# Ungated weight loads, half tile loads as single steps, first v ahead of the identities, and a written-out order in an RWKV-5 attention and squared-ReLU kernel

## The chip, the cores and the metric

One core of a Trainium2 chip. The metric is device time in microseconds, from the start to the end of one execution; lower is better.

## The reference

```python
# r, k, v: (4, 8, 768, 48) f32; w, u: (8, 48); moe_w_in: (384, 2048); moe_w_out: (2048, 384)
state = zeros((B, H, D, D))
for t in range(S):
    cur = einsum('bhd,bhe->bhde', u * k[:, :, t], v[:, :, t])
    y[:, :, t] = einsum('bhd,bhde->bhe', r[:, :, t], state + cur)
    state = w[:, :, None] * state + einsum('bhd,bhe->bhde', k[:, :, t], v[:, :, t])
x = y.transpose(0, 2, 1, 3).reshape(B * S, H * D)     # 3072 x 384
out = (relu(x @ moe_w_in) ** 2) @ moe_w_out           # 3072 x 384
```

A linear attention with a decaying state, and behind it a two-layer network with a squared ReLU.

## The kernel before

The sequence is cut into 6 chunks of 128 positions. A unit is one chunk of one of the 4 batches, so there are 24 units, numbered chunk by chunk: unit i is chunk i // 4 of batch i % 4. A chunk's attention is done by matrix products instead of the recurrence. The steps of a unit, by the names of the program's planner:

- `rt`, `kt`, `vt`: loads of the unit's tile of r, k and v (192 KB each). The loads of r and k are issued by SP, those of v by POOL. For units 0 to 5 the tiles of r and k come in two halves with longer rows.
- `scale` (DVE, L458 and L460): r and k times powers of w, into the padded tile rkw.
- `turn` (PE transposes, L487) and `rkT` (ACT copies, L494), or from unit 6 on one transposing DMA (L476): rkT. `kb` (PE, L502, then ACT) turns k back for units 0 to 5. `vb` (ACT, L471) casts v.
- `rk` (DVE, L513), `at` (PE, L521) and `mask` (DVE, L533): the scores. `s` (called `sums` in the old code; PE, L541 and L546): the diagonal sums and the unit's share of the state. `dv`, `sadd`, `sdec` (DVE) and `stb` (ACT): diagonal term and state.
- `y` (PE, L576 and L582), `yb` (DVE, L591): the unit's y. `xturn` (PE, L607) and `xT` (ACT, L611), or from unit 6 on a transposing DMA (L600): x turned.
- `m1(i, s)` (PE, L623): quarter s of x @ w_in for unit i, 12 matmuls; needs quarter s of w_in, called I0 to I3 here. `relu` (ACT, L631), `sq` (ACT L638 or DVE L640). `m2(i, q)` (PE, L647): quarter q of the second product, 4 matmuls; needs quarter q of w_out, O0 to O3. `osb` (ACT, L654), `out` (SP): result and store.

Every weight quarter is loaded by POOL with a cast to bf16 (384 KB as bf16). Before its issue, POOL makes a one-column copy (`gate`, L442) of a tile of r or k that it is gated by, so the issue waits until that tile has landed: I0 by kt(2), I1 by rt(2), I2 by rt(4), I3 by kt(3), O3 by kt(4), O0 by rt(3), O1 by rt(4), O2 by kt(2). v(i) is gated in the same way by kt(i - 1) from unit 2 on (L465). POOL also makes the two identity matrices, at the very start (before the first v), the mask (`upper`), zeros, and the columns for u and the state's decay (`uwb`, `wend`).

The order on each engine is found when the program is built: `Plan` holds each step with an engine, a cost, a rank and the steps that it needs, and walks through a modelled time, giving each engine the step of lowest rank that is ready. It also gives out the 8 PSUM banks, and puts short matmuls on a constant tile (`fill`, L380) where PE would have nothing to do early on, 98 of them. Each engine then carries out its list in order.

On POOL the order is: v0, upper, v1, zeros, uwb, v2, I0, v3, I1, wend, I3, I2, v4, O0, O1, O2, O3, v5, v6 and so on. On PE, the order around the first products is: turn(3,1), m1(0,0), s(2), m1(1,0), y(2), kb(3), turn(4,0), at(3), s(3), xturn(2), m1(0,1), m1(1,1), m1(2,1), y(3), m1(2,0), turn(4,1), m1(0,3), ... and the second product begins m2(0,0), m1(3,1), m1(3,2), xturn(4), m2(1,0), m2(0,1), ..., m2(0,2), m1(4,3), m2(1,1), m2(1,2), m2(0,3).

Of the kernel before, what the change touches and what calls it, by code (L numbers as in the profile page):

```python
# [16 lines left out]
class Plan:  # L17

    def __init__(self, lags, cold, spare, turns):
        self.turns = turns
        self.lags = lags
        self.cold = cold  # L30
        self.spare = spare
        self.steps = []
        self.at = {}
        self.users = {}
        self.place = {}

    def add(self, key, engine, cost, emit, needs=(), rank=0.0, new=(), uses=(), move=None):
        kind, which = (key[0], key[1] if len(key) == 2 else key[1:]) if isinstance(key, tuple) else ("", key)
        rank = self.turns.get(kind, {}).get(which, rank)
        s = dict(key=key, engine=engine, cost=cost, emit=emit, rank=rank, new=new, move=move)  # L40
        s["needs"] = [n for n in needs if n is not None]
        self.at[key] = s
        self.steps.append(s)
        for x in tuple(new) + tuple(uses):
            self.users.setdefault(x, []).append(s)

    def run(self, room, banks, count):
        todo = {}
        for s in self.steps:
            todo.setdefault(s["engine"], []).append(s)  # L50
        for mine in todo.values():
            mine.sort(key=lambda s: s["rank"])
        rings = {name: [] for name in room}
        free = {e: 0.0 for e in todo}
        queues = {e: [] for e in todo}
        held = {n: None for n in range(count)}
        since = {n: 0.0 for n in range(count)}
        begin, until, tight, loose = self.spare
        free["SP"] = 0.74
        held[0] = "fill"  # L60
        order = []
        t = 0.0
        left = len(self.steps)
        tiny = 1e-9

        moved, chained, left_pe, to_pe, near = self.lags

        def ready(s, e):
            if s["move"]:
                return s["end"] + moved + s["move"][4]  # L70
            if s["engine"] == "PE":
                return s["end"] + (chained if e == "PE" else left_pe)
            return s["end"] + (to_pe if e == "PE" else near)

        marks = []

        def mark(s):
            for e in ("PE", ""):
                heappush(marks, ready(s, e))

        def done(s, e):
            return "end" in s and ready(s, e) <= t + tiny

        def fits(s):
            e = s["engine"]
            names = [x[0] for x in s["new"]]
            for name in set(names):
                if name in banks:
                    continue
                ring, m = rings[name], room[name]  # L90
                for n in range(len(ring) - m, len(ring) - m + names.count(name)):
                    if n >= 0 and not all(done(x, e) for x in self.users[ring[n]]):
                        return False
            wanted = [name for name in names if name in banks]
            if wanted:
                for n, x in held.items():
                    if x not in (None, "fill") and all(done(u, e) for u in self.users[x]):
                        held[n], since[n] = None, max(u["end"] for u in self.users[x])
                if sum(x is None for x in held.values()) < len(wanted):
                    return False  # L100
                for name in set(wanted):
                    mine = sum(x is not None and x[0] == name for x in held.values())
                    if mine + wanted.count(name) > banks[name]:
                        return False
            return True

        while left:
            if held[0] == "fill" and t > until:
                held[0] = None
            for e, mine in todo.items():  # L110
                if free[e] > t + tiny:
                    continue
                if e == "PE" and t < begin - tiny:
                    free[e] = begin
                    continue
                for s in mine:
                    if s["move"] and sum(x[1] / x[0]["move"][0] * x[0]["move"][3] for x in queues[e]) > 1.5:
                        continue
                    if all(done(self.at[k], e) for k in s["needs"]) and fits(s):
                        mine.remove(s)  # L120
                        left -= 1
                        for x in s["new"]:
                            if x[0] in banks:
                                n = 4 + x[1] if x[0] == "log" else min((n for n in held if held[n] is None), key=lambda n: since[n])
                                held[n] = x
                                self.place[x] = n
                            else:
                                rings[x[0]].append(x)
                        s["start"] = t
                        free[e] = t + s["cost"] * (self.cold[1] if e == "PE" and t < self.cold[0] else 1.0)  # L130
                        if s["move"]:
                            queues[e].append([s, s["move"][0], free[e] + s["move"][2]])
                        else:
                            s["end"] = free[e]
                            mark(s)
                        order.append(s)
                        break
                else:
                    if e == "PE" and t < until:
                        free[e] = t + (tight * self.cold[1] if t < self.cold[0] else loose)  # L140
                        order.append(dict(key="fill", emit=self.fill, start=t, end=free[e], engine="PE"))
            heads = [q[0] for q in queues.values() if q]
            moving = [x for x in heads if x[2] <= t + tiny]
            whole = sum(x[0]["move"][1] for x in moving)
            later = [f for f in free.values() if f > t + tiny]
            while marks and marks[0] <= t + tiny:
                heappop(marks)
            later += marks[:1]
            later += [x[2] for x in heads if x[2] > t + tiny]
            later += [t + x[1] * whole / x[0]["move"][1] for x in moving]  # L150
            if not later:
                if left:
                    raise ValueError("nothing can go on: " + str([s["key"] for m in todo.values() for s in m[:3]]))
                break
            step = min(later) - t
            t += step
            for x in moving:
                x[1] -= step * x[0]["move"][1] / whole
                if x[1] <= 1e-7:
                    queues[x[0]["engine"]].pop(0)  # L160
                    x[0]["end"] = t
                    mark(x[0])
        return order
# [3 lines left out]
def kernel(  # L167
# [26 lines left out]
    LATE = (0.2, 0.2, 0.4)  # L194
    MOST = 3
    SQUARES = 'AAAMAAAM'
    TURNS = {
        "": {
            "zeros": 38.551
        },  # L200
        "O": {
            0: 76.019, 1: 91.228, 2: 107.535, 3: 7
        },
        "rt": {
            0: -83.003, 1: -66.162, 12: 22.377, 13: 28.231, 14: 28.49, 15: 33.657, 3: -36.29, 5: 1.476, 8: 3.237
        },
        "kt": {
            0: -80.584, 1: -55.486, 10: 19.508, 11: 20.529, 2: -47.443, 6: 2.358
        },
        "at": {  # L210
            0: -3.958, 11: 34.671, 4: -16.745, 7: 10.944
        },
        "mask": {
            (1, 0): -39.238, (10, 0): 33.02, (2, 1): 25.375, (5, 1): 1.515
        },
        "sadd": {
            1: 9.124, 4: 45.244
        },
        "rk": {
            2: 13.012, 7: 14.32, 8: 68.867, 9: -12.042  # L220
        },
        "sums": {
            11: 49.353, 2: -24.778, 8: 5.082
        },
        "dv": {
            2: -26.848, 7: 34.164, 9: -12.993
        },
        "stb": {
            2: -9.741, 4: 57.421
        },  # L230
        "scale": {
            (10, 0): 23.594, (11, 0): -15.371, (3, 0): -29.763, (4, 0): 33.082, (7, 1): 6.517, (8, 1): 4.379
        },
# [656 lines left out]
```

## Time and profile before

| | |
|---|---|
| time, median of 3 runs | 175.78 us (175.55 to 176.24) |
| span of the profiled execution | 174.3 us (its own time beyond the span is not given; the median stands 1.5 us above the span) |
| PE busy | 166.7 us, 96% |
| ACT / DVE / POOL busy | 132.1 / 121.1 / 40.0 us |
| granted TensorE clock | 1.000 |
| DMA | 28.93 MB; HBM read 20.50 MB, written 4.72 MB |

How to read the lines of the profile: times are microseconds from the start of the span. In the chain of waits, each line is a start, a length, and what the chain was in. In a timeline, a line is a start, a length, the engine and line, the operation with the output and the inputs, and in brackets the idle time before it and what ended it. A row of the busy time by stretches is the stretch, its length, then the busy time and the count of instructions of PE, PEld (weight loads), DVE, ACT and POOL, then the clock, the DMA share and GB/s. A row of a DMA queue is its number of packets, megabytes written, and the time of its packets as a share of the 16 DMA engines' time in the stretch; shares of two queues can sum to over 100%. q0 is POOL's queue, q1 that of SP. "DMA to landing" is the time from an issue to its last byte, the three numbers being equal where the stretch holds a single issue.

### The profile page before, as it was taken

Reading aid. Unit: us, or ns where it says so; the run is one execution under the profiler, and the core shown is the slowest. Engines: PE = TensorE matmul, PEld = TensorE weight load, DVE = VectorE, ACT = ScalarE, POOL = GpSimd, SP = SyncE. Lnnn points to the kernel's source line nnn. Section 1 sums busy time; section 2 is a strip of 40 time slices with the busy share of each in tenths; the row PEclk is TensorE's granted clock in tenths of the full one; section 3 lists DMA queues with packets and bytes.
Section 4 is the critical chain, followed back from the end, with each engine's and each line's share of the span. In section 5 each row is a group of like instructions: output and inputs, shape, how many; then the busy total and the mean of one; then the engine's idle time right before and its main releaser. Section 6 shows DMA issues by size and latency. Waiting matters only on the chain.

```text
span 174.3 us, 5795 instructions
## 1 busy us (share of the span) xinstructions
PE 166.7 (96%) x2390; PEld 134.7 (77%) x2390; DVE 121.1 (70%) x252; ACT 132.1 (76%) x268; POOL 40.0 (23%) x84
## 2 busy tenths in 40 slices
PE   7978899999999999999999999999999999999991
PEld 6766799887687787886896787869787698877871
DVE  7869976615999899977986799794989635531010
ACT  3946999999458797886968876939994869948640
POOL 7866890300140220302032202203202000000000
PEclk9999999999999999999999999999999999999999
DMA  4889999999999999999999999999999971130121
GB/s 97 228 179 246 232 218 193 185 221 118 170 201 164 178 154 209 200 214 170 231 142 183 156 237 214 218 177 141 186 200 175 271 180 26 26 111 6 47 81 56
DMA packets 76474, 28.93 MB, mean 166 GB/s; under 512 B 65440, under 2 KB 75296, under 8 KB 76448
## 3 DMA queue, kind: packets, MB, share of 16 engines
q1 hardware_dynamic: 70848, 20.56, 69.8%
q0 software_dynamic: 5312, 7.87, 23.9%
q8 instruction: 18, 0.29, 0.8%
q10 hardware_dynamic: 288, 0.15, 0.4%
q14 instruction: 8, 0.07, 0.1%
HBM read 20.50 MB, written 4.72 MB: 145 GB/s over the span
## 4 chain that ended last, share of the span: by engine, by line
PE 81%; DMA 11%; SPq 4%; issue 1%; DVE 0%; POOL 0%; POOLq 0%
PE bank L623 35%; PE bank L647 33%; DMA w_in_q<-in_moe_w_in_dram 5%; SPq L436 4%; DMA rkT<-rkw 4%; PE bank L521 4%; DMA rt<-in_r_dram 2%; PE bank L576 2%; PE bank L582 2%; PE bank L546 2%; PE bank L663 2%; PE bank L541 1%; PE bank L487 0%; PE bank L607 0%; POOL gate L442 0%
## 5 line engine op out<-in xcount | busy, mean ns | idle before, releaser
L623 PE MATMUL bank<-xT,w_in_q 128*128 128x128 bf16 x1152 | 70.7, 219 | 0.1
L623 PEld LDWEIGHTS <-w_in_q 128*128 128x128 bf16 x1152 | 66.5, 98 | 3.1 <-DMA w_in_q<-in_moe_w_in_dram 0.3
L647 PE MATMUL bank<-w_out_q,g 128*128 128x384 bf16 x368 | 66.9, 326 | 0.0
L631 ACT ACTIVATE gr<-bank 128x512 f32<-128x512 f32 x96 | 54.3, 599 | 13.6 <-PE bank L623 13.3
L647 PEld LDWEIGHTS <-g 128*128 128x128 bf16 x368 | 33.3, 98 | 19.8
L638 ACT ACTIVATE g<-gr 128x512 bf16<-128x512 f32 x72 | 43.7, 637 | 0.4
L533 DVE TENSOR_TENSOR am<-bank,smask 128x512 bf16<-128x512 f32 x48 | 31.3, 682 | 3.3 <-PE bank L521 3.1
L640 DVE TENSOR_TENSOR g<-gr 128x512 bf16<-128x512 f32 x24 | 16.5, 686 | 21.5 <-ACT gr L631 21.5
L465 POOL COPY gate<-kt 128x1 f32<-128x1 f32 x22 | 5.8, 266 | 80.9 <-DMA kt<-in_k_dram 80.9
L654 ACT COPY osb<-bank 128x384 f32<-128x384 f32 x23 | 11.0, 483 | 15.8 <-PE bank L647 15.8
L467 POOL DMA_DIRECT2D vt<-in_v_dram x24 | 21.4, 893 | 5.9 <-issue 1.6
L555 DVE TENSOR_TENSOR dv<-vb,bank 128x384 f32<-128x384 bf16 x24 | 13.2, 548 | 5.3 <-PE bank L546 3.4
L513 DVE TENSOR_TENSOR rk<-rkT 128x512 bf16<-128x512 bf16 x24 | 10.0, 417 | 7.7 <-DMA rkT<-rkw 4.3
L591 DVE TENSOR_TENSOR yb<-bank,dv 128x384 bf16<-128x384 f32 x24 | 13.2, 550 | 2.8 <-PE bank L582 2.4
L471 ACT CAST vb<-vt 128x384 bf16<-128x384 f32 x24 | 12.4, 518 | 0.0
L458 DVE TENSOR_TENSOR rkw<-rt,wpos 128x384 bf16<-128x384 f32 x18 | 9.8, 550 | 1.4 <-DMA rt<-in_r_dram 1.4
L458 DVE TENSOR_TENSOR rkw<-kt,wneg 128x384 bf16<-128x384 f32 x18 | 9.9, 549 | 0.9 <-DMA kt<-in_k_dram 0.9
L567 ACT CAST stb<-st 128x384 bf16<-128x384 f32 x20 | 10.4, 519 | 0.0
L380 PE MATMUL bank<-warm 128*128 128x128 bf16 x98 | 9.3, 248 | 1.1 <-DVE warm L322 1.1
L521 PE MATMUL bank<-rkT 64*128 64x128 bf16 x192 | 9.5, 219 | 0.2
L494 ACT COPY rkT<-bank 128x512 bf16<-128x512 bf16 x12 | 6.8, 588 | 3.0 <-PE bank L487 3.0
L563 DVE TENSOR_TENSOR st<-st,wend 128x384 f32<-128x384 f32 x16 | 8.8, 549 | 0.0
(74 smaller groups left out, 129.1 us busy)
## 6 DMA issues: line engine op xcount, KB each, us to landing
vt<-in_v_dram POOLq DMA_DIRECT2D x24, 192.0 KB, 4.6
out_dram<-osb SPq DMA_DIRECT2D x23, 192.0 KB, 4.0
rt<-in_r_dram SPq DMA_DIRECT2D x18, 192.0 KB, 4.5
kt<-in_k_dram SPq DMA_DIRECT2D x18, 192.0 KB, 4.3
w_in_q<-in_moe_w_in_dram POOLq DMA_DIRECT2D x4, 384.0 KB, 7.9
w_out_q<-in_moe_w_out_dram POOLq DMA_DIRECT2D x4, 384.0 KB, 12.7
kt<-in_k_dram SPq DMA_DIRECT2D x12, 96.0 KB, 4.3
rt<-in_r_dram SPq DMA_DIRECT2D x11, 96.0 KB, 4.2
```

Source lines behind the costliest of these rows:

```text
L458: nc.vector.tensor_tensor(t["rkw"][:, x, :, :, :D], pair(src), pair(wneg if x else wpos), ALU.mult)
L467: nc.gpsimd.dma_start(out=tiles[i]["vt"], in_=v[b, :, c * C : (c + 1) * C, :].rearrange("h s d -> s h d"))
L471: nc.scalar.copy(tiles[i]["vb"], tiles[i]["vt"])
L521: nc.tensor.matmul(out=t["at"][o][:, p, :], lhsT=t["rkT"][sl, 1, p, :], rhs=t["rkT"][sl, 0, p, :], start=True, stop=True,)
L533: nc.vector.tensor_tensor(am, t["at"][o], smask.unsqueeze(1).to_broadcast([C, HP, C]), ALU.mult)
L555: nc.vector.tensor_tensor(t["dv"], t["vb"], t["d"].unsqueeze(2).to_broadcast([C, H, D]), ALU.mult)
L591: nc.vector.tensor_tensor(t["yb"], t["y"], t["dv"].rearrange("p h d -> p (h d)"), ALU.add)
L623: nc.tensor.matmul(out=t["h", s][:, a], lhsT=turned, rhs=chunks[c]["xT"][:, n, b : b + m, :], start=(n == 0), stop=(n == NK - 1),)
L631: nc.scalar.activation(t["gr", s], t["h", s], AF.Relu)
L638: nc.scalar.activation(g, x, AF.Square)
L640: nc.vector.tensor_tensor(g, x, x, ALU.mult)
L647: nc.tensor.matmul(out=t["o"], lhsT=chunks[units[i][0]]["g"][:, f, units[i][1], :], rhs=w_out_q[f // 4][:, f % 4, :], start=(f == 0), stop ...
```

## The change

- The planner is gone. The order of all steps is written out in a table of words, each step with the PSUM bank or banks that it takes (`m1.0.0@4`); each engine runs its words in the order of the table. 99 fills stand in it.
- The weight quarters have no gates. The order on POOL is v0, v1, the identities, I3, upper, I0, zeros, I2, uwb, wend, I1, v2, v3, O0, O3, O1, v4, v5, O2, v6 and so on. v is gated by the k before it from unit 6 on (`VGATE`), not from unit 2 on.
- A half tile load of r or k is a step of its own (`kt.0.0`), so that halves of different tiles can stand in any order: kt(0) comes first on SP, then rt(0,0), rt(1), rt(2), kt(1,1), kt(2), rt(3) and so on. kt(1,0) is issued from ACT's queue.
- The identities are made behind v(0) and v(1) on POOL, not ahead of them.
- On PE, unit 0 takes its four quarters early: turn(2,1), m1(0,0), s(1), kb(2), y(1), turn(3,0), at(2), m1(0,3), m1(0,2), turn(3,1), xturn(1), m1(0,1), at(3), kb(3), m1(1,2), m1(1,3), y(2), s(2), m1(1,1), y(3), s(3), turn(4,0), turn(4,1), m1(1,0), m2(0,0), xturn(3), at(4), xturn(2), kb(4), m1(3,0), ... m2(1,0), ... m2(1,1), y(4), turn(5,1), s(4), m2(0,1), m1(2,3), m2(1,2) ... Ahead of m1(0,0) stand turn(1,1), at(1), xturn(0) and kb(1). Later units' steps are also reordered throughout, for example unit 18's first product behind that of unit 21. Counts of steps ahead of and behind a step, here and below, are taken from the two orders.

```diff
+ORDER = """
+kt.0.0 kt.0.1 rt.0.0 rt.1.0 vt.0 rt.1.1 fill.25 log@4567 ktA.1.0 lnat.0 vt.1 rt.2.0 lnat.1 w.0 rt.2.1 ids w.1
+scale.0.0 kt.1.1 wk scale.0.1 I.3 kt.2.0 wr fill.16 turn.0.0@1 upper kt.2.1 turn.0.1@2 rkT.0.0 cols@3 scale.1.0
+rt.3.0 vb.0 I.0 copied rkT.0.1 rt.3.1 fill.6 turn.1.0@4 zeros vb.1 rk.0 kt.3.0 fill.6 kb.0@5 rkT.1.0 I.2 at.0@67
+kbT.0 kt.3.1 scale.2.0 uwb end mask.0.0 kt.4.0 fill.12 turn.2.0@1 mask.0.1 kt.4.1 wend rkT.2.0 scale.1.1 fill.8
+s.0@3 fill.1 y.0@2 dv.0 I.1 fill.4 turn.1.1@4 sadd.0 rt.4.0 rkT.1.1 vt.2 yb.0 stb.0 rk.1 rt.4.1 fill.14 at.1@56
+scale.2.1 vt.3 xturn.0@7 mask.1.0 kb.1@1 xT.0 rt.5.0 fill.2 turn.2.1@3 O.0 kbT.1 mask.1.1 rkT.2.1 fill.5 m1.0.0@4
+O.3 scale.3.0 rt.5.1 s.1@2 rk.2 relu.0.0 kb.2@7 O.1 sadd.1 y.1@5 rt.6 turn.3.0@1 kbT.2 at.2@06 dv.1 sqA.0.0 vt.4
...
+"""
-class Plan:
...
-    ident4 = const.tile([HP, HP], F32)
-    make_identity(nc, ident4)
...
+    def identities():
+        make_identity(nc, ident4)
+        make_identity(nc, identb)
...
-    def load(i, name):
+    def load(name, i, o=None, queue=None):
...
+        if o is None:
+            nc.sync.dma_start(out=t[name], in_=src.rearrange("h s d -> s h d"))
+        else:
+            (queue or nc.sync).dma_start(out=t[name][:, o * 4 : o * 4 + 4].rearrange("p l d -> p (l d)"), in_=halves(src)[o])
-    def weights(gated, q, which):
-        nc.gpsimd.tensor_copy(gate, tiles[gated[1]][gated[0]][:, H - 1, :1])
+    def weights(which, q):
...
     def load_v(i):
-        if i > 1:
+        if i >= VGATE:
             nc.gpsimd.tensor_copy(gate, tiles[i - 1]["kt"][:, H - 1, :1])
...
+    for word in ORDER.split():
+        what, _, where = word.partition("@")
+        name, *a = what.split(".")
+        if name == "fill":
+            for _ in range(int(a[0])):
+                fill()
+            continue
+        a = [int(x) for x in a]
+        if where:
+            place.update(zip(names(name, *a), (int(x) for x in where)))
+        steps[name](*a)
```

More of the change, by code (lines that the diff above doesn't have):

```diff
@@ L1 @@
 from contextlib import ExitStack
-from heapq import heappop, heappush
 import concourse.bass as bass
@@ L14 @@
 PSUM = bass.MemoryType.PSUM
-class Plan:
[L27 to L163, printed above, removed]
@@ new lines @@
+vb.6 kt.8 xturn.4@2 sqD.2.3 at.5@43 xT.4 m2.1.3 vt.7 scale.6.1 sqA.2.0 mask.5.1 m1.3.1@1 vb.5 osb.1 mask.5.0 m2.0.3
+rkD.6 sqA.3.0 scale.8.0 out.1 m2.2.0@5 relu.3.1 stb.4 y.5@7 osb.0 m2.2.1 scale.7.1 vt.8 sqA.3.1 out.0 m2.3.0@2 rkD.7
+vb.7 m2.2.2 s.5@3 kt.9 m2.3.1 dv.5 m1.4.0@0 sadd.5 vt.9 scale.8.1 m1.4.3@4 relu.4.0 sdec.5 m1.4.2@1 yb.5 sqA.4.0
+rk.6 rkD.8 at.6@63 relu.4.3 xturn.5@0 vb.8 mask.6.0 m2.3.2 relu.4.2 sqD.4.3 m2.3.3 xT.5 mask.6.1 stb.5 m2.2.3 osb.3
+sqA.4.2 m1.5.2@7 rt.9 osb.2 m2.4.0@4 out.3 relu.5.2 out.2 y.6@6 vb.9 rk.7 rt.10 at.7@10 sqA.5.2 m1.5.0@3 mask.7.0
@@ L166 @@
+osb.20 m2.18.1 out.20 m2.18.2 m2.18.3 m2.22.0@5 osb.18 m2.22.1 out.18 m2.22.2 m2.22.3 m2.23.0@1 osb.22 out.22
+m2.23.1@2 osb.23.0 out.23.0 osb.23.1 out.23.1
+"""
 @with_exitstack
@@ L300, in bank @@
             banks.extend([late.tile([128, 512], F32, name=f"bank{n}") for n in range(4, 8)])
-        return banks[plan.place[key]]
+        return banks[place[key]]
     ET = mybir.EngineType
@@ L331 @@
     ident4 = const.tile([HP, HP], F32)
-    make_identity(nc, ident4)
+    identb = const.tile([128, 128], BF16)
     which = const.tile([128, 2], I32)
@@ L683, in store @@
         nc.sync.dma_start(out=out[b * S + c * C : b * S + (c + 1) * C, :], in_=tiles[i]["osb"])
-    PE, ACT, DVE, POOL, SP = "PE", "ACT", "DVE", "POOL", "SP"
-    L1, L2 = 7, 18
-    def late(n, i):
-        return min(MOST, LATE[n] * max(0, i - NPE))
-    def do(fn, *a):
-        return lambda: fn(*a)
-    add = copy = plan.add
-    plan.fill = fill
-    add("w0", ACT, 3.2, None, rank=-1e3)
-    add("log", PE, 0.28, spread_log, rank=-1e3, needs=["w0"], new=[("log", n) for n in range(4)])
-    for x in range(2):
-        add(("lnat", x), DVE, 0.47, do(log_at, x), rank=-1e3 + x, needs=["w0", ("lnat", 0) if x else None])
-        add(("w", x), ACT, 0.42, do(power_four, x), rank=-1e3 + x, needs=[("lnat", x)])
@@ L704 @@
-    add("wk", ACT, 0.48, do(power, wneg, down), rank=-999, needs=["log", ("w", 1)], uses=[("log", n) for n in range(4)])
-    add("wr", ACT, 0.48, do(power, wpos, up), rank=-998, needs=["wk"], uses=[("log", n) for n in range(4)])
-    add("wu", POOL, 3.85, None, rank=-1e3)
-    add("upper", POOL, 0.9, upper, rank=-998, needs=["wu"])
-    add("zeros", POOL, 0.5, zeros, rank=-996, needs=["upper"])
-    add("cols", PE, 0.15, spread_columns, rank=-50, needs=["upper"], new=[("h", "cols")])
-    add("copied", DVE, 0.1, copy_columns, rank=-50, needs=["cols"], uses=[("h", "cols")])
@@ L854, with names @@
-    room = dict(
-        rt=7, kt=7, vt=7, rkw=NPAD, g=2, rkT=6, vb=NVB, rk=4, am=8, dv=4, yb=4, xT=3, gr=6, osb=6,
-    )
-    for s in plan.run(room, dict(at=4, s=2, y=2, h=5, o=2, log=4), 8):
-        if s["emit"] is not None:
-            s["emit"]()
+    def names(name, *a):
+        if name == "log":
+            return [("log", n) for n in range(4)]
+        if name == "at":
+            return [("at", a[0], o) for o in range(2)]
+        if name == "m2":
+            return [("o", *a)] if a[0] == NU - 1 else [("o", a[0])]
+        if name in ("s", "y"):
+            return [(name, *a)]
+        return [dict(cols=("h", "cols"), turn=("h", a[0], "rk", *a[1:]), kb=("h", *a[:1], "kb"), xturn=("h", *a, "x"), m1=("h", *a))[name]] if a else [("h", "cols")]
@@ new lines @@
+    steps = dict(
+        log=spread_log, lnat=log_at, w=power_four, wk=lambda: power(wneg, down), wr=lambda: power(wpos, up),
+        ids=identities, upper=upper, zeros=zeros, cols=spread_columns, copied=copy_columns, uwb=u_columns,
+        end=end_columns, wend=end_blocks, I=lambda q: weights("I", q), O=lambda q: weights("O", q),
+        rt=lambda *a: load("rt", *a), kt=lambda *a: load("kt", *a), ktA=lambda *a: load("kt", *a, nc.scalar), rtA=lambda *a: load("rt", *a, nc.scalar),
+        vt=load_v, vb=cast_v, scale=scale, turn=turn, rkT=lambda i, x=None: evict_rk(i, x), rkD=turn_dma, kb=turn_back, kbT=evict_back,
+        rk=rk, at=at, mask=mask, s=sums, dv=diag_v, sadd=state_add, sdec=state_decay, stb=state_cast,
+        y=y_mm, yb=evict_y, xturn=x_turn, xT=evict_x, xD=x_dma,
+        m1=lambda i, s: mm1(i, 1, s), relu=lambda i, s: relu(i, 1, s),
+        sqA=lambda i, s: square(i, 1, s, True), sqD=lambda i, s: square(i, 1, s, False),
+        m2=lambda i, q: mm2(i, q) if i < NU - 1 else mm2_half(i, q),
+        osb=lambda i, n=None: evict_o(i) if n is None else evict_half(i, n),
+        out=lambda i, n=None: store(i) if n is None else store_half(i, n),
+    )
```

304 lines of the change are left out of this document (59 added, 245 removed).

## The prediction

> **What bounds the kernel now.** I read the page's busy times first, then the busy time by stretches of ten microseconds, then the chain of waits in order of time.
>
> ```profile
> span 174.3 us, 5795 instructions
> PE 166.7 (96%) x2390; PEld 134.7 (77%) x2390; DVE 121.1 (70%) x252; ACT 132.1 (76%) x268; POOL 40.0 (23%) x84
> ...
> 30.00:40.00 10.00, 10.00 (x133) 8.19 (x131) 4.80 (x9) 9.96 (x22) 1.55 (x2) 1.00 1.24 200
> ...
> 21.96 2.18 PE bank L623 x36
> ...
> 38.19 2.60 PE bank L647 x16
> ...
> 49.49 0.17 PE bank L607 x3
> 49.66 0.08 PE bank L541 x4
> 49.74 0.19 PE bank L546 x4
> 49.93 0.65 PE bank L647 x4
> ...
> 51.25 0.20 PE bank L576 x8
> 51.45 0.17 PE bank L582 x4
> 51.62 0.67 PE bank L623 x12
> 52.29 0.33 PE bank L521 x8
> ...
> 168.08 2.65 PE bank L663 x32
> 170.76 0.29 DVE osb L675
> ```
>
> PE is the bound. From 21.96 on the chain is PE work almost without a break until 168.08 + 2.65 = 170.73, and a stretch from the middle (30 to 40) has PE busy for all of its 10 us. Behind 170.73 come the last eviction and store, 174.3 - 170.73 = 3.6 us, which the change leaves as they are. So no order of the work behind 22 us can make PE's part much shorter. What can move is (a) when PE gets something to do in the head, and (b) holes that a new order opens later. The single rows are the prices of steps: m1 0.67, m2 0.65, at 0.33, s 0.08 + 0.19, y 0.20 (and 0.17 more from the second chunk on), xturn 0.17; a turn or a kb, four transposes, is priced at 0.22 from the next fence.
>
> What held PE until 21.96:
>
> ```profile
> 5.44 0.40 PE L487 MATMUL bank<-identb,rkw 128*128 128x128 bf16 x4
> ...
> 8.76 0.24 PE L541 MATMUL bank<-uwb,rk 128*128 128x8 bf16 x4
> ...
> 11.45 0.48 ACT L611 COPY xT<-bank 128x384 bf16<-128x384 bf16 x1 [0.32 <-PE bank L607]
> ...
> 17.56 0.83 PE L623 MATMUL bank<-xT,w_in_q 128*128 128x128 bf16 x12
> ...
> 21.96 2.01 PEld L623 LDWEIGHTS <-w_in_q 128*128 128x128 bf16 x36 [0.27 <-DMA w_in_q<-in_moe_w_in_dram]
> ...
> 25.02 0.22 PE bank L487 x4
> ```
>
> The first x of unit 0 is ready at 11.93, but m1(0,0) runs at 17.56, and at 21.96 m1(0,1) starts when quarter 1 of w_in lands. The weights are what comes last, so removing their gates aims at the right place.
>
> **The change, part by part.** How fast POOL's own queue (q0: v and the weights) and SP's queue (q1) move is read from the DMA view in three stretches, 4 to 12, 12 to 22 and 22 to 40 us; megabytes, then share of the 16 engines' time:
>
> ```profile
> q1 hardware_dynamic: 1623, 1.11, 57.9%
> q0 software_dynamic: 196, 0.59, 25.8%
> ...
> q0 software_dynamic: 1064, 1.19, 69.9%
> q1 hardware_dynamic: 2270, 1.05, 42.7%
> ...
> q0 software_dynamic: 2950, 2.90, 90.5%
> q1 hardware_dynamic: 3371, 0.70, 31.9%
> ```
>
> With weights queued, q0 moves 0.119 MB/us beside SP's half loads (12 to 22) and 0.161 MB/us beside the later, finer loads (22 to 40). While its weights were gated, it moved 0.074 (4 to 12). That gap is what the change can win.
>
> Which bytes must be there is read from two landings, each an issue and its time to landing: the third weight issue and the sixth v.
>
> ```profile
> 17.13 0.78 POOL L445 DMA_DIRECT2D w_in_q<-in_moe_w_in_dram  x1 [0.27 <-issue]
> DMA to landing us min/median/max: 7.5/7.5/7.5
> ...
> 24.07 0.90 POOL L467 DMA_DIRECT2D vt<-in_v_dram  x1
> DMA to landing us min/median/max: 15.8/15.8/15.8
> ```
>
> At 17.13 + 7.5 = 24.6 q0 had delivered v(0) to v(3) and three quarters, 4 x 192 + 3 x 384 = 1920 KB. At 24.07 + 15.8 = 39.9 it had delivered v(0) to v(5) and all eight quarters, 4224 KB. The changed POOL order is v0, v1, I3, I0, I2, I1, v2, v3, O0, O3, O1, v4, v5, O2. Its I1 completes the same 1920 KB (2 x 192 + 4 x 384), and its O2 the same 4224 KB. If q0 runs s us ahead of before, I1 lands at 24.6 - s and O2 at 39.9 - s.
>
> Now what PE has left behind each. In the old order m1(0,1) started at 21.96 with 170.73 - 21.96 = 148.8 us of PE work. Counted in the two orders from that step on, the new one has one m1 fewer, but one at, one y, two s, one xturn, one turn and one kb more: -0.67 + 0.33 + 0.20 + 0.54 + 0.17 + 0.22 + 0.22 = +1.0. So PE's end is at least (24.6 - s) + 149.8 = 174.4 - s, and the old 170.73 is met at s = 3.7. The last weight quarter is harsher. In the old order its first user was m2(0,3), which ran at 38.19 + 2 x 0.65 = 39.5, with 131.2 left. In the new order it is m2(1,2), with four m1, two m2 and one xturn more and two turns fewer to come: +2.68 + 1.30 + 0.17 - 0.44 = 3.7, so 134.9 left. PE's end is at least (39.9 - s) + 134.9 = 174.8 - s, and the old end is met only at s = 4.1. The new order asks for the whole set of weights 4 us sooner, relative to its end, than the old one did; unless the queue gains 4 us, this term decides.
>
> How large is s? Between 4 and 12 us q0 at its 12-to-22 rate would move 8 x 0.119 = 0.95 MB instead of 0.59, so +0.36. v(0) ahead of the identities goes out 0.8 us sooner:
>
> ```profile
> 2.30 0.61 POOL L330 DMA_DIRECT2D wu<-in_u_dram  x1
> ...
> 3.46 0.29 POOL masks.py:199 TENSOR_SCALAR_AFFINE_SELECT identb<-identb 128x128 bf16<-128x128 bf16 x1
> ...
> 3.70 0.93 POOL L467 DMA_DIRECT2D vt<-in_v_dram  x1
> ```
>
> (3.70 against 2.30 + 0.61 = 2.91), worth 0.8 x 0.119 = 0.10 MB. Together 0.46 MB, and at the rate that holds when O2 is moved, 0.46 / 0.161 = 2.9 us. PE's end: 174.8 - 2.9 = 171.9, 1.2 us later than 170.73. The ends of s: if SP's loads keep q0 at 0.074 until 12, only the 0.10 MB is won, s = 0.6 and PE ends at 174.2 (+3.5). If q0 took 0.161 from 4 to 22, it would move 2.90 instead of 1.78 MB, s = (1.12 + 0.13) / 0.161 = 7.8, and another term takes over, m1(0,0), below. I take 2.9 because the 12-to-22 stretch is the nearest row: weights beside the same half loads.
>
> Against the removal of gates stands a rule of the Trainium skill, page "DMA: Bandwidth & Descriptors", section "Rules for kernel authors": queues fed from different engines run on the same 16 DMA engines and interleave, so spreading brings no bandwidth. By it alone, ungated weights would only take from SP's loads; the rows leave some room all the same, 57.9 + 25.8 = 84% in use before 12 us against 69.9 + 42.7 = 113% after.
>
> The other edits:
> - Identities behind v(0) and v(1). identb ends at 2.91 + 2 x 0.93 + 0.84 = 5.6 instead of 3.75 (the four identity steps took 2.91 to 3.75), and the first transposes, which ran at 5.44, slip by 0.2. uwb, which s(0) needs, now stands behind I3, upper, I0, zeros and I2 on POOL. At no more than 0.93 for each of the five and for uwb (the longest POOL row here) it is done by 5.6 + 6 x 0.93 = 11.2; s(0) slips from 8.76 by 2.4 at most, and x(0) from 11.93 to 14.4. The cover is the wait for weights until I1: m1(0,0) could start at 14.5, and with the 4.6 us of steps that the new order has beyond the old count of 148.8 (1.0 as above and 3.6 between m1(0,0) and m1(0,1)) PE would end at 14.5 + 153.4 = 167.9. So this costs nothing while s is below 174.8 - 167.9 = 6.9.
> - kt(1,0) on ACT's queue: one DMA issue of about 0.62 us ahead of the first Exp. ACT was idle for 0.62 there anyway, and each load behind it on SP goes out one issue sooner; nothing on the path.
>
> ```profile
> 1.41 0.62 ACTq L319 DMA_DIRECT2D rt<-in_r_dram  x1
> ...
> 4.26 1.11 ACT L402 ACTIVATE wfour<-lnat 128x384 f32<-128x384 f32 x2 [0.62 <-DVE lnat L397]
> ...
> L591 DVE TENSOR_TENSOR yb<-bank,dv 128x384 bf16<-128x384 f32 x24 | 13.2, 550 | 2.8 <-PE bank L582 2.4
> ...
> xT<-yb SPq DMA_TRANSPOSE x18, 4.1
> ```
>
> - Twelve gate copies go (eight weights, v(2) to v(5)). POOL is busy 23%: nothing by themselves.
> - The table. PE's total work is the same set of steps, and 99 fills stand where 98 did. The distance from y to the first m1 of a unit, which must hold a DVE add (0.55), a transpose by DMA (4.1 to landing) and SP's place in line, falls from at least 7.2 us of PE work (units 6 and later) to 6.1 at unit 22 and 6.2 at unit 7. That still holds the 4.65, with about 1.5 us for SP's line instead of 2.6. I put 0 on it and keep up to 2 us for the top of the range.
>
> Sum: 174.3 + 1.2 = 175.5 of span. The median of the runs, 175.78, stands 1.5 above the span of the profiled execution; with that, **177.0 us**.
>
> **Rivals.**
> *The queue wins more than 4 us.* If q0 and q1 took turns packet for packet in the head as they nearly do from 22 to 40 (2950 against 3371), q0 would gain there. A q0 packet takes 160 us x 0.699 / 1064 = 105 ns in 12 to 22, a q1 packet 30 ns. A round of one and 2.13 costs 169 ns, of one and one 135, so 0.119 becomes 0.149 MB/us: over 4 to 22 us 2.68 MB plus 0.12 instead of 1.78, s = 6.3, PE's end 168.5 and 173.5 us. At the bound of m1(0,0) it would be 167.9 and 173.0. For it: the even packets of the later stretch. Against it: 1064 against 2270 in the head, where q1 takes two for one. The Trainium skill, same page, "Queues, rings and completion order", says that an engine goes round the queues packet by packet; by that rule this rival's 173.5 would hold, and the head's row does not bear it out.
> *Nothing measurable.* s close to 4.1: the start wins what the earlier need for weights loses. For it: DMA had 29 points of its share idle before 12 us; all of them given to q0 at its own 0.59 MB for 25.8 points would be +0.66 + 0.10 MB, s = 4.7 and PE's end 170.1, 175.1 us, the near edge of this case; the far edge is 176.6.
> *The order's tight places open as well.* Beside O2, the shorter y-to-m1 distances and the SP line, where transposes stand behind stores that wait for evictions: at a wait of 1 to 2 us once or twice, PE's end moves to 173 to 174.5, 178 to 179.6 us. It decides once SP's line is later than the 1.5 us of room. For it: PE takes its steps in order, and the distances shrank; against it: the room of 1.5 us is still there, and the old trace shows PE without a break at its own close places.
> *The head's loads starve.* kt(1,1) must arrive for turn(1,1), which now stands ahead of xturn(0); it counts only if m1(0,0) slips past 171.9 - 153.4 = 18.5, 4 us behind its latest time above. Unlikely, and inside the range.
>
> **How the numbers follow.** Forecast (O2 late, 176.7 to 178): 0.40. More than 4 us won: 0.24. Nothing measurable: 0.20. Tight places or starved loads: 0.16. What a measurement of this kernel can tell from no change is 0.5%, 0.9 us: faster 0.24, same 0.20, slower 0.56. The range leaves a tenth at each side: at the bottom to the turn-taking rival, 173.5, at the top to the end of s with SP's loads first, 3.5 above 175.78, 179.3.
>
> **What would show it.** Right: in the changed profile PE waits at L623 for w_in_q near 20 to 22 us and at the m2 matmuls for w_out_q near 37; PE's last matmul ends near 172. Wrong: no wait of PE for w_out_q at all and I1 landed by 18 us (the first rival), or PE idle behind 45 us on transposes (the third).

## The result, and the profile after

The changed kernel takes 182.12 us (median of 4 runs, 180.49 to 184.24); in the same session the kernel before took 175.82 us. The ratio is 1.033, 95% interval 1.027 to 1.039: slower, and above the forecast range of 173.5 to 179.3. Ratios, here and below, are of runs in the faster of two states; medians and ranges hold all runs, here a slow one of 184.24 us too. The profiled execution is the run of 180.49 us.

The page of the changed kernel and PE's last step in its chain of waits (start, length, what the chain was in):

```profile
span 178.7 us, 5772 instructions
PE 166.4 (93%) x2391; PEld 134.8 (75%) x2391; DVE 120.7 (68%) x252; ACT 132.9 (74%) x268; POOL 39.3 (22%) x72
...
172.34 2.65 PE bank L492 x32
```

PE's busy time is that of before (166.4 against 166.7), but its last matmul ends at 172.34 + 2.65 = 174.99 instead of 170.73. The 4.26 us are idle time of PE. PE's timeline shows where; the number in the brackets is the idle time just before the row, with what ended it:

```profile
15.64 0.84 PE L452 MATMUL bank<-xT,w_in_q 128*128 128x128 bf16 x12 [0.98 <-DMA w_in_q<-in_moe_w_in_dram]
...
21.20 0.84 PE L452 MATMUL bank<-xT,w_in_q 128*128 128x128 bf16 x12 [1.19 <-DMA w_in_q<-in_moe_w_in_dram]
...
40.87 0.82 PE L476 MATMUL bank<-w_out_q,g 128*128 128x384 bf16 x4 [0.50 <-ACT g L467]
...
87.10 1.50 PE L452 MATMUL bank<-xT,w_in_q 128*128 128x128 bf16 x24 [0.87 <-DMA xT<-yb]
...
101.68 1.51 PE L452 MATMUL bank<-xT,w_in_q 128*128 128x128 bf16 x24 [2.07 <-DMA xT<-yb]
...
113.72 2.17 PE L452 MATMUL bank<-xT,w_in_q 128*128 128x128 bf16 x36 [0.29 <-DMA xT<-yb]
```

The first two rows are m1(0,0) and m1(0,1), which wait for weight quarters, as forecast. The other rows are what the forecast put at nothing: holes behind 40 us, in a stretch where the old trace has PE without a break. Three of them are an m1 that waits for its transposing DMA (x of units 10, 13 and 15). The waits of PE behind 30 us, summed (line, releaser: us, times, longest):

```profile
PE bank L452 <- DMA xT<-yb: 3.2, 3, 2.1
PE bank L476 <- ACT g L467: 0.5, 1, 0.5
PE bank L354 <- DMA rkT<-rkw: 0.3, 1, 0.3
```

That is 4.0 of the 4.26 us. The rest is the head, whose landings are two issues of POOL, I1 and O2, each with its time to landing:

```profile
DMA to landing us min/median/max: 9.9/9.9/9.9
...
21.43 0.76 POOL L281 DMA_DIRECT2D w_out_q<-in_moe_w_out_dram  x1 [2.03 <-DMA w_in_q<-in_moe_w_in_dram]
DMA to landing us min/median/max: 14.5/14.5/14.5
```

I1, issued at 11.26, landed at 21.2 and was waited for. O2 landed at 21.43 + 14.5 = 35.9, and no m2 waited for a quarter of w_out: of the whole head, only m1(0,1) at 21.20 is on the path. With 149.8 us of PE work behind it (the prediction's count) PE would have ended at 171.0, only 0.3 later than before.

### The profile page after: what moved, and what is told of

It reads as the page before. It is cut to its first block, busy times and chain, and to the rows that moved or that the text cites. A ratio compares the mean times of both kernels' runs of the same rounds, so it can differ in the third digit from the quotient of the medians.

```text
span 178.7 us, 5772 instructions
## 1 busy us (share of the span) xinstructions
PE 166.4 (93%) x2391; PEld 134.8 (75%) x2391; DVE 120.7 (68%) x252; ACT 132.9 (74%) x268; POOL 39.3 (22%) x72
## 5 line engine op out<-in xcount | busy, mean ns | idle before, releaser
L452 PE MATMUL bank<-xT,w_in_q 128*128 128x128 bf16 x1152 | 73.1, 219 | 5.4 <-DMA xT<-yb 3.2
L467 ACT ACTIVATE g<-gr 128x512 bf16<-128x512 f32 x72 | 44.5, 639 | 0.7
L298 POOL COPY gate<-kt 128x1 f32<-128x1 f32 x18 | 6.7, 372 | 82.2 <-DMA kt<-in_k_dram 82.1
L483 ACT COPY osb<-bank 128x384 f32<-128x384 f32 x23 | 11.1, 484 | 10.4 <-PE bank L476 10.4
L354 PE MATMUL bank<-rkT 64*128 64x128 bf16 x192 | 9.0, 218 | 0.3 <-DMA rkT<-rkw 0.3
L388 DVE TENSOR_TENSOR st<-bank,st 128x384 f32<-128x384 f32 x16 | 8.7, 548 | 0.8 <-PE bank L375 0.8
L405 PE MATMUL bank<-vb,am 128*128 128x48 bf16 x192 | 8.7, 183 | 0.0
```

The source lines that it names most:

```text
L452: nc.tensor.matmul(out=t["h", s][:, a], lhsT=turned, rhs=chunks[c]["xT"][:, n, b : b + m, :], start=(n == 0), stop=(n == NK - 1),)
L467: nc.scalar.activation(g, x, AF.Square)
L483: nc.scalar.copy(tiles[i]["osb"], tiles[i]["o"])
```

## The experiments

All are made from the changed kernel's table of words; a diff shows words that move. Each was timed in three rounds against the kernel before (medians of 175.3 to 175.5 us in those sessions).

**Is it the place of the x transposes on SP's line, or the head?** Four kernels of one session. The first moves the transposes of x(10) and x(13) ahead of the loads and the store that stood just before them on SP:

```diff
-kt.14 ... kt.15 ... out.8 ... xD.10
+xD.10 kt.14 kt.15 out.8
-kt.17 ... kt.18 ... xD.13
+xD.13 kt.17 kt.18
```

> The changed kernel, but on SP's queue the transposing DMA of x(10) goes ahead of the loads kt(14), kt(15) and the store of unit 8, and that of x(13) ahead of kt(17) and kt(18). Theory A (PE's late holes come from the loads that stand ahead of x's transposes on SP's queue): the holes of 0.87 us at 86.2 and 2.07 us at 99.6 close, the span falls by 2 to 3 us from 178.7 to about 176, unless the next transposes take their place. Theory B (the transposes land late because all 16 DMA engines are full, wherever they stand in the line): they land as late as before, span 178 to 179.

Measured: 183.22 us (181.49 to 185.34), ratio 1.034 (1.029 to 1.040). In its profiled execution, the longest of its runs, no m1 waits for x any more, but the time is in another hole, ahead of at(15). The rows are the rk transpose that it waits for, with its time to landing, and the hole:

```profile
89.86 1.33 SPq L309 DMA_TRANSPOSE rkT<-rkw  x1
...
DMA to landing us min/median/max: 11.4/11.4/11.4
...
101.30 1.03 PE L354 MATMUL bank<-rkT 64*128 64x128 bf16 x16 [4.67 <-DMA rkT<-rkw]
```

This rk transpose went out at 89.86, ahead of the transposes of x(12) and x(13), so SP's line did not hold it back: its landing took 11.4 us, those of the two behind it 7.3 and 10.4. That is nearer to theory B. The place on SP's line is not a cure by itself.

The second puts m1(0,1) behind work that doesn't need I1:

```diff
-m1.0.1 ... at.3 ... kb.3 ... m1.1.2 ... m1.1.3
+at.3 kb.3 m1.1.2 m1.1.3 ... m1.0.1
```

> The changed kernel, but m1(0,1), which waited 1.2 us for w_in's quarter 1, runs behind at(3), kb(3), m1(1,2) and m1(1,3) on PE. If the landing of that quarter sets where PE's gapless part begins, PE's end and the time fall by 0.7 to 1.2 us. If the late holes are set by transposes that depend on DMA and not on PE, the gain is eaten there and the time stays within 0.5 us.

Measured: 180.68 us (177.76 to 181.52), ratio 1.019 (1.008 to 1.030). The head's weight wait shrinks from 1.2 to nothing at m1(0,1) (0.6 is left at m1(0,0)), but 0.7 and 0.6 appear at rkT and vb. The interval of the ratio overlaps that of the changed kernel, so a gain isn't shown. Of the late holes the largest stays, and it is longer:

```profile
101.80 2.48 PE L452 MATMUL bank<-xT,w_in_q 128*128 128x128 bf16 x24 [2.51 <-DMA xT<-yb]
```

The third and the fourth keep the order that the planner of before wrote, put into the table. One has only the gates of the weights and of v(2) to v(5) gone; the other has the changed kernel's order on POOL besides.

```diff
 (order of before)
-gates on I0-I3, O0-O3, v2-v5
```

> The old order of every engine, written out as a table; the only edits are that the gate copies ahead of the eight weight quarters and of v(2) to v(5) are gone, and the identities are made in the same place as before. Theory A (the loss lies in the new order; weights without gates are worth something by themselves): no late holes, faster than the kernel before by 1 to 3 us, 173 to 175 us. Theory C (weights without gates starve the loads of r and k, and the late holes follow from that): slower than before, 177 us or more, with PE waiting for scale or transposes behind 17 us.

Measured: 177.47 us (175.12 to 178.48, 10 runs), ratio 1.006 (1.002 to 1.011). The profiled execution is the longest of the ten.

```diff
 (order of before, no gates)
-POOL: v0 ids upper v1 zeros uwb v2 I0 v3 I1 wend I3 I2 v4 ...
+POOL: v0 v1 ids I0 upper I1 zeros I3 ... uwb ... wend I2 v2 v3 O0 O1 v4 ...
```

> As the one before it, and POOL's order is like the changed kernel's: v0, v1, identities, I0, upper, I1, zeros, I3, uwb, wend, I2, v2, v3, O0, O1, v4, O2, O3, v5. Theory A: I1 lands at 15 to 17 us instead of 21.9, and PE begins its gapless part as soon as the loads allow; 172 to 175 us. Theory C: slower than the run before it, as r and k come later still, 177 us or more.

Measured: 181.9 us (181.33 to 182.37), ratio 1.036 (1.032 to 1.040). PE's longest waits behind 8 us, first in the kernel before, then without gates, then with POOL's order as well:

```profile
13.80 0.62 PE L487 MATMUL bank<-identb,rkw 128*128 128x128 bf16 x8 [1.90 <-DVE rkw L460]
```

```profile
13.79 0.62 PE L321 MATMUL bank<-identb,rkw 128*128 128x128 bf16 x8 [1.52 <-DVE rkw L294]
```

```profile
17.28 0.87 PE L321 MATMUL bank<-identb,rkw 128*128 128x128 bf16 x8 [4.01 <-DVE rkw L294]
```

All three wait for a half of r to land and be scaled. The kernel before has this wait too, so the removal of the gates alone does not make it; POOL's order on top of it makes it 2.1 us longer, and it ends 3.5 us later. There, weights that go out early take from these loads: the halves of r and of k took 4.2 and 4.3 us to landing before (medians), 4.0 and 4.8 with only the gates gone, 7.9 and 6.8 with POOL's order too, and 7.8 and 8.2 in the changed kernel. With only the gates gone, PE no longer waits for I1, but m1(0,1) runs at 22.34 instead of 21.96, behind a new wait of 0.56 us for a half of k. The changed table's order on SP and PE fits the ungated head (its PE has no such hole behind 12 us); the old order with the ungated queue doesn't. Ungating alone brings no gain.

**Is it a debt of DMA work, or the table's tail?** In the changed kernel the DMA share falls to 0.70 between 50 and 60 us (0.98 before), while SP stands at xD.7 with loads behind it. Theory D of the next expectations takes the late holes as the price of that gap. The first kernel fills it:

```diff
-xD.7 ... xD.6 ... rt.12 ... rt.13 ... kt.10
+rt.12 rt.13 kt.10 xD.7 ... xD.6
```

> The changed kernel with one thing moved on SP's line: the loads rt.12, rt.13 and kt.10 go out ahead of the transposing DMA xD.7 instead of behind xD.6. Theory D (the table's SP line stands from about 52 to 54.8 us at xD.7 with loads behind it that nothing holds, the DMA share between 50 and 60 falls to 0.70 from 0.98, and what was not moved there is missing until 115): the share between 50 and 60 rises to 0.9 or more, the three late holes of 1.5, 1.5 and 2.2 us ahead of the m1 rounds (waits on DMA xT<-yb) shrink by some 2 to 3 us together, PE ends near 172.5, profile span near 176. Rival P (the holes come from how late yb is computed and from what is queued just ahead of each xD, not from a debt): holes as in the changed kernel within 1 us, span 178 to 179.5.

Measured: 181.19 us (178.53 to 183.67), ratio 1.024 (1.014 to 1.033). Stretches of the changed kernel, then of this one (us, length, busy PE, PEld, DVE, ACT, POOL, clock, DMA share, GB/s), and two holes of this kernel, ahead of unit 7's first m1 and of m1(13,0):

```profile
50.00:60.00 10.00, 10.00 (x151) 7.80 (x147) 8.37 (x18) 7.66 (x15) 0.88 (x1) 1.00 0.70 140
```

```profile
50.00:60.00 10.00, 9.53 (x140) 7.42 (x139) 8.56 (x18) 7.50 (x15) 0.89 (x2) 1.00 1.00 179
...
60.18 2.84 PE L452 MATMUL bank<-xT,w_in_q 128*128 128x128 bf16 x48 [0.65 <-DMA xT<-yb]
...
102.49 1.51 PE L452 MATMUL bank<-xT,w_in_q 128*128 128x128 bf16 x24 [2.07 <-DMA xT<-yb]
```

(The expectations of this group put the changed kernel's three late holes at 1.5, 1.5 and 2.2 us, 5.2 in all; PE's timeline has 0.87, 2.07 and 0.29, 3.2 in all.) The gap is filled, 0.70 to 1.00, and the hole ahead of m1(13,0) is the same to the hundredth. A new one of 0.65 us opens at 60.18: with the loads ahead of it, unit 7's transpose goes out at 57.12 instead of 54.80. The waits for x come to 3.5 us. Theory D falls by these holes; the interval of the ratio overlaps that of the changed kernel.

The second lightens the DMA engines:

```diff
-    nc.sync.dma_start(out=out[... : b * S + (c + 1) * C, :], in_=tiles[i]["osb"])
+    n = 32 if i < 12 else C
+    nc.sync.dma_start(out=out[... : b * S + c * C + n, :], in_=tiles[i]["osb"][:n])
```

> The changed kernel, but the stores of units 0 to 11 write 32 of their 128 rows (left out: three quarters of those rows of the output; all arithmetic is done). It frees DMA of some 9 stores' worth from 40 to 115 us. Theory D and any other theory by which the late holes are a matter of how much the 16 DMA engines have to carry: the x transposes land within about 4.5 us of their issue, the three late holes are below 1 us together, PE ends near 171.5, span near 175. Rival P (yb late, order on SP's line, PE's own order): the holes stay within 1 us of 5.2 in all.

Measured: 178.57 us (176.42 to 178.96), ratio 1.018 (1.014 to 1.022). In the profiled execution (176.42) PE waits for nothing but this behind 18 us:

```profile
PE bank L452 <- DMA w_in_q<-in_moe_w_in_dram: 1.2, 1, 1.2
PE bank L476 <- ACT g L467: 0.8, 1, 0.8
```

The x holes are gone, and between 84 and 112 us the median landing of an x transpose is 5.2 us instead of the changed kernel's 6.5. The other runs are some 2 us longer; where, no trace shows. So what the DMA engines have to carry there is one half of the cause. It is not what the change brought: in this stretch the DMA share is 1.21 in the changed kernel and 1.25 before, where PE has no hole. The other half is the order. The third kernel has the table up to xD.7 and then what is left in the order, and with the banks, of before:

```diff
 (the changed table up to yb.6)
-xD.7 m2.5.1 sadd.6 ... (its tail)
+sqA.4.1 m2.4.1 m2.4.2 ... xD.6 ... xD.7 ... (the tail of before)
```

> The changed kernel up to xD.7 (about 52 us), and from there all that is left in the order, and with the banks, that the planner of before wrote. If the late holes come from what the new table has behind that point (its places of xD.6, xD.7, xD.10, xD.13, xD.14), they go: PE idle behind 55 us under 1 us, PE ends 171 to 172, span about 175.5. If they are the price of the changed head (a DMA debt and late v loads that any order meets later), they stay, 3 to 4 us, at other places: span 178 to 179.

Measured: 177.69 us (177.37 to 178.81), ratio 1.014 (1.009 to 1.018). PE's waits behind 18 us:

```profile
PE bank L452 <- DMA w_in_q<-in_moe_w_in_dram: 1.7, 1, 1.7
PE bank L476 <- ACT g L467: 0.7, 1, 0.7
PE bank L370 <- DVE rk L346: 0.3, 1, 0.3
```

No wait for x, with the full stores and the changed head. Of the 3.3% that the change lost, 1.9 points are in its tail (ratio 1.033 against 1.014). The last of the four is fill_gap with m1(0,1) moved as above.

> fill_gap together with m1(0,1) behind at(3), kb(3), m1(1,2) and m1(1,3) on PE (as in m1_later, whose head waited 0.6 us less). Theory D: the gains add: PE ends near 172, median near 177, some 5 us under the changed kernel and about 1 us over the kernel before. Rival P: as m1_later, 180 to 181.

Measured: 182.63 us (182.19 to 183.71), ratio 1.042 (1.037 to 1.046). The pieces don't add: the x holes stay, and waits that the head had covered come out.

```profile
PE bank L452 <- DMA xT<-yb: 3.8, 4, 2.1
PE bank L354 <- DMA rkT<-rkw: 1.6, 1, 1.6
PE bank L405 <- ACT vb L304: 1.2, 2, 0.6
PE bank L354 <- ACT rkT L327: 0.9, 2, 0.6
```

**The distance.** What differs in the tail is the PE work that the order leaves between y and the first m1 of a unit (all such distances here, in the prediction and in the expectations count y's own 0.37 us). In before it is 10.5, 13.1 and 13.1 us for units 10, 13 and 15; in the change 7.2, 6.6 and 9.6, and these are the three units with holes (0.87, 2.07 and 0.29 us). Theory E: a hole opens where this work is less than x's way from y to its landing. The next kernel lengthens it for unit 13 alone, by letting unit 12's first product go first:

```diff
-m1.12.0 m1.13.0 m1.13.1 ... m1.13.2 ... m1.13.3 ... m1.12.1 m1.12.3 m1.12.2
+m1.12.0 m1.12.3 m1.12.1 ... m1.12.2 ... m1.13.0 ... m1.13.3 m1.13.1 m1.13.2
```

(relu, squares, m2, osb and the stores of the two units move with them.)

> The changed kernel with one stretch of the table rewritten: three of the m1 steps of unit 12 (whose transpose is long there) stand where m1(13,0), m1(13,1) and m1(13,2) stood, and those go behind; the PE work between y(13) and its first m1 rises from 6.6 to 10.9 us, nothing else moves. Theory E (a hole opens where the PE work that the order leaves between y and the first m1 of a unit is less than the way of x: DVE add, SP's line, and a transpose that takes 5.5 to 7.5 us to land where the DMA engines are full): the hole of 2.07 us ahead of m1(13,0) goes, no other opens by more than 1 us, PE ends 173 to 173.5, median 178.5 to 181. Theory F (DMA is the bound between 60 and 115 and the order only decides where PE stands for it): the 2 us come back as a hole at the next x or rk transpose, before 116, and PE ends at 175 as in the changed kernel.

Measured: 179.67 us (179.22 to 183.56), ratio 1.023 (1.017 to 1.029). The profiled execution is the one of 183.56 us, which waited 3.2 us for a quarter of w_in in its head, so only its waits behind 30 us are read:

```profile
PE bank L476 <- DVE g L469: 1.4, 2, 0.8
PE bank L452 <- DMA xT<-yb: 1.0, 3, 0.6
```

The hole ahead of m1(13,0) is gone, and waits for x fall from 3.2 to 1.0 us. A part of the time comes back, at squares that the swap brought close to their m2 (1.4 us), and not at the next transpose, where theory F had put it. The ratio is lower than the changed kernel's 1.033, but the intervals still touch.

The converse, on old_tail: unit 13's first three m1 go ahead of the last three of unit 12, and the distance falls from 13.1 to 7.3 us.

```diff
-m1.12.0 m1.12.1 m1.12.2 m1.12.3 ... m1.13.0 m1.13.1 m1.13.2 m1.13.3
+m1.12.0 m1.13.0 m1.13.1 m1.13.2 ... m1.12.1 m1.12.2 m1.12.3 m1.13.3
```

(relu and squares of the two units move with them.)

> The converse, in old_tail (the order of before from xD.7 on, no hole there): m1(13,0), m1(13,1) and m1(13,2) are pulled ahead of the last three m1 steps of unit 12, which brings the PE work between y(13) and its first m1 from 13.1 to 7.3 us. Theory E: a hole of 0.5 to 2 us opens ahead of m1(13,0), waiting for DMA xT<-yb, near 99 us, and the kernel is that much slower than old_tail (178.2 to 179.7). Rival (the distance isn't what matters; the rest of the new table is): no hole, 177.7 as old_tail.

Measured: 182.69 us (181.47 to 185.58), ratio 1.041 (1.033 to 1.050) against old_tail's 1.014, and above the 178.2 to 179.7 of theory E. Unit 13's yb on DVE, its x transpose on SP with the time to landing, and the hole:

```profile
90.78 0.55 DVE L420 TENSOR_TENSOR yb<-bank,dv 128x384 bf16<-128x384 f32 x1
...
95.59 1.25 SPq L429 DMA_TRANSPOSE xT<-yb  x1
...
DMA to landing us min/median/max: 4.0/4.0/4.0
...
99.61 3.71 PE L452 MATMUL bank<-xT,w_in_q 128*128 128x128 bf16 x36 [2.48 <-DMA xT<-yb]
```

One move of three steps in an order that had no hole opens one of 2.48 us, where theory E put one of 0.5 to 2, and costs more than its length: PE ends at 176.30 instead of 172.64 in the profiled executions, 3.7 us later. The last section shows why. Here SP's line is what is long (91.33 to 95.59), in the changed kernel the landing.

Last, old_tail with m1(0,1) behind the same four steps as in m1_later, the best of the pieces:

> old_tail, with m1(0,1) behind at(3), kb(3), m1(1,2) and m1(1,3) on PE as in m1_later: the best of the pieces seen so far. If the wait of 1.7 us for the second weight quarter in the head falls to about 0.6 us and the tail stays without holes: some 1 us under old_tail, 176.5 to 177, still above the kernel before (175.3 to 175.8), because the ungated head lets PE start on the weights no earlier in sum. If other waits take its place in the head (as in fill_later, 0.6 us at each of rkT and vb): 177.5 to 178.

Measured: 178.31 us (178.09 to 178.36), ratio 1.016 (1.011 to 1.021): just above the second of the two outcomes written down, and not told from old_tail (1.009 to 1.018). The wait for I1 goes, and these stand in its place:

```profile
PE bank L354 <- ACT rkT L327: 0.9, 2, 0.7
...
PE bank L405 <- ACT vb L304: 0.6, 1, 0.6
```

No version found beats the kernel before.

## Why the prediction was wrong

**The bound** was right: PE's busy time did not change, and each us of idle time on PE behind 22 us is a us of the kernel.

**The head** was right in mechanism, mis-sized by 0.9 us. The forecast took s, by which POOL's queue runs ahead, as 2.9 us. It was 24.6 - 21.2 = 3.4 for I1 and 39.9 - 35.9 = 4.0 for O2. By the prediction's own sums PE's end is then 171.0 by I1 and 174.8 - 4.0 = 170.8 by O2: the term that decided is the other one, and the head lost 0.3 us instead of 1.2. That the announced wait for w_out near 37 us isn't there says the same.

**The rival by which the queue wins more than 4 us** was right in its rate, where both queues were full. Packets, megabytes and DMA share of the changed kernel, 4 to 12 and 12 to 22 us:

```profile
q0 software_dynamic: 675, 0.92, 62.3%
q1 hardware_dynamic: 1170, 0.80, 39.3%
...
q0 software_dynamic: 1275, 1.49, 79.5%
q1 hardware_dynamic: 1240, 0.85, 36.7%
```

From 12 to 22 the packets are one to one and q0 moves 0.149 MB/us, the rival's number. The Trainium skill, page "DMA: Bandwidth & Descriptors", section "Queues, rings and completion order", has each DMA engine go round its queues packet by packet; here the trace agrees, 1275 against 1240. From 4 to 12, with weights issued only from 5.88 on, q0 moved 0.115 MB/us, so by 22 us the gain over before is 0.33 + 0.30 = 0.63 MB, 3.9 us at 0.161, not 6.3; O2 gained 4.0. The 0.8 us by which v(0) goes out sooner, which the forecast counted as 0.10 MB and this rival as 0.12, give nothing beside that: q0 moved 0.00 MB before 4 us in both kernels. And the time would not have followed: the tail decides.

**The table is the step that failed.** "I put 0 on it and keep up to 2 us for the top of the range." It cost 4.0 us of PE's holes in the profiled execution. The test was the right one, the distance from y to the first m1 against the way of x, but three things in it were wrong. The distances count y's own matmuls, 0.37 us, which are over before the DVE add can start, so the least room was 1.1 us, not 1.5. The way was priced with the median landing of all 18 transposes, 4.1 us, and the smallest distances (units 7 and 22) were looked at, not those where the transposes land late. Between 84 and 112 us the median landing is 6.5 us in the changed kernel, and was 5.6 before, where the range over all 18 is 2.4 to 6.3 us; the old trace had these rows:

```profile
xT<-yb SPq DMA_TRANSPOSE x5, 6.5
```

```profile
xT<-yb SPq DMA_TRANSPOSE x4, 5.6
```

Unit 13's way in the changed kernel: y's last matmuls, yb on DVE, the issue on SP, the landing.

```profile
93.06 0.33 PE L411 MATMUL bank<-stb,rkT 128*128 128x96 bf16 x4
...
93.66 0.55 DVE L420 TENSOR_TENSOR yb<-bank,dv 128x384 bf16<-128x384 f32 x1
...
94.75 3.15 SPq L429 DMA_TRANSPOSE xT<-yb  x1
...
DMA to landing us min/median/max: 6.9/6.9/6.9
```

93.39 to 101.65 is 8.3 us. Of the 6.6 us that the order leaves, y's own apart, there are 6.2 behind 93.39; PE was through with that by 99.6 and waited 2.07. The line on SP took 0.54 us, well within the room. The landing took the rest: 6.9 instead of 4.1. The two shortest distances, unit 22's 6.1 us and unit 7's 6.2, have no hole. The transposes of units 7 and 6 landed so:

```profile
DMA to landing us min/median/max: 2.4/2.8/3.3
```

They went out in the stretch with a DMA share of 0.70, but in fill_gap, with 1.00 there, they land in 2.3 to 3.0 us all the same. So the share alone does not tell how long a landing takes; what else does is open.

**The rival of the order's tight places** was the right one, at 0.16 for it and the starved loads together. Its place (an m1 that waits for x) and its size (1 to 2 us, once or twice) are what the profile shows; its point of decision, SP's line, was not the one reached, and its 178 to 179.6 lies below the median of 182.12. The waits were three, and by PE's 4.26 us alone the time comes to 175.78 + 4.26 = 180.0, near the profiled run's 180.49; the other runs are longer, and a hole can cost more than its length, which no term had.

**The starved halves** of r and k, an unlikely case of the prediction, decide with the old order on SP and PE once POOL's order is the new one (4.0 us of wait, where before has 1.9). The changed table avoids that, and this is the part of it that works.

What remains of the loss without the tail is in old_tail: its PE ends at 169.84 + 2.80 = 172.64, 1.9 us behind before. Its m1(0,1) ran at 21.77, which with 149.8 of work is 171.6, and the two waits of 0.74 and 0.3 us are the rest.

```profile
21.77 0.84 PE L452 MATMUL bank<-xT,w_in_q 128*128 128x128 bf16 x12 [1.68 <-DMA w_in_q<-in_moe_w_in_dram]
...
169.84 2.80 PE L492 MATMUL bank<-w_out_q,g 128*128 128x256 bf16 x32
```

Open: why the runs of the changed kernel spread over 4 us. The two longest have a mean clock of 0.981 and 0.988, the two shortest 1.000. That their hole grew past the length at which the clock falls, as below, fits this, but they have no trace.

## What to carry to other kernels

Price a transfer by its landing in the stretch where it will run, not by the median over the kernel, and set the whole way (producer, place in the queue, landing) against the work that the order puts between producer and consumer, for each unit. A bound engine without slack needs only a few us of that work too little to lose all that an earlier start can win, and more than its idle time if the clock falls behind the hole. Taking a gate away mostly moves bytes: of the 0.64 MB that POOL's queue moved more by 22 us (2.42 against 1.78), 0.41 came out of the loads on SP's and ACT's queues (2.10 against 2.51). Look for the loads that now come later, and rearrange their users too.

## What the runs showed of the hardware that was not expected

**A hole of PE of 2.5 us halves the clock behind it.** In old_tail_m1_13, the stretches behind the hole of 2.48 us:

```profile
99.60:101.00 1.40, 1.39 (x14) 1.40 (x15) 0.00 (x0) 0.00 (x0) 0.10 (x1) 0.50 0.96 249
101.00:102.00 1.00, 1.00 (x12) 1.00 (x11) 0.00 (x0) 0.60 (x1) 0.00 (x0) 0.50 1.16 291
...
103.00:104.00 1.00, 1.00 (x28) 0.94 (x26) 0.30 (x1) 1.00 (x3) 0.00 (x0) 1.00 0.35 46
```

The granted clock is 0.50 for some 3 us (0.58 from 102 to 103, where it comes back), and 36 matmuls of m1 take 3.71 us instead of 2.17 (the row at 113.72 above): 1.5 us on top of the 2.48. The same stands behind the holes of 2.51 (m1_later), 3.22 (m1_13_later, in its head), 4.01 (old_pool) and 4.67 us (x_first). Behind 2.07 us in the changed kernel and in fill_gap the clock stayed at 1.00; no hole here lies between 2.07 and 2.48. The Trainium skill, page "TensorE: Matmul & The Clock Gate", section "Part 1: The HAM clock gate (the "warmup" mystery)", puts the fall to half behind at least one idle window of about 3.4 us; here less was enough, and the measurement decides.

**POOL's queue holds itself without gates.** POOL's issues, with the wait before them:

```profile
18.52 0.89 POOL L300 DMA_DIRECT2D vt<-in_v_dram  x1 [1.52 <-DMA w_in_q<-in_moe_w_in_dram]
```

v(5) waited until I2 had landed, and O2 until I1 had (its row is in the first section). Both times eight loads of POOL were under way. Whether the chip or the program's own waits set this, no run shows. The written order asked for O2 some 2 us before it could go out.
